# Layer two's last two query chunks of two tiles joined into one of four, with a second wide mixer buffer and new planning constants

## The chip, the cores and the metric

The kernel runs on one core of a Trainium2 chip. The metric is the time of one execution in device microseconds (us), less is better. A run is quoted as the median of its executions with their range. The span that a profile shows is of one of these executions (for the kernel before, of a further one), and about 1.8 us shorter than its timed value. The profiler also records the **granted clock** of TensorE, as a share of full speed: 1.00 or, for some microseconds at a time, 0.50.

## The reference, cut to what matters

```python
# x: 1 x 2048 x 448, bf16; 16 heads of 28; F = 1792
def _A_ref(x, wqkv, wo):                      # attention, all keys visible
    ...
    scores = einsum("bhqd,bhkd->bhqk", q, k) * Dh ** -0.5
    p = softmax(scores); o = einsum("bhqk,bhkd->bhqd", p, v)
    return o @ wo
def _B_ref(x, w1, w2, w3, w4):                # "mixer"
    h = gelu(layernorm(x) @ w1)
    # four quarters of h shifted by +1, -1, +2, -2 rows of the sequence
    x1 = x + concat(shifted quarters) @ w2
    return x1 + gelu(layernorm(x1) @ w3) @ w4
# twice: x = x + A(layernorm(x)); x = x + B(layernorm(x))
```

The sequence is 16 tiles of 128 rows. The row shifts are why a tile can be mixed only when its neighbour's attention is done: tiles 11-12 need tile 13.

## The kernel before

A list scheduler in Python plans every instruction before the kernel is built. Tasks (generators) offer operations with an assumed duration; the planner places each on its engine by priority and by the time at which it believes the inputs to be ready. **The order on each engine is fixed then.**

The softmax is a stream: TensorE writes score blocks into PSUM (the memory for its results, in eight banks), ScalarE takes two or three banks per exponential (1024 or 1536 columns), TensorE multiplies the result with the values. VectorE evaluates some 40 of the 2048 blocks itself with a polynomial. Projections and mixers are hidden beside this stream. What depends on the last query chunk comes after the last exponential; I call that the **tail**, and the end of the last exponential **T**.

```python
CHUNKS = {0: [...], 1: [(0, 4), (4, 4), (8, 4), (12, 2), (14, 2)]}    # (first tile, tiles) of query chunks, by layer
BGROUPS = {0: [...], 1: [[[0, 1, 2]], [[3, 4, 5, 6]], [[7, 8, 9, 10]], [[11, 12]], [[13, 14, 15]]]}  # mixers after each chunk
RANK = {...}      # order list of the hidden tasks
D_RATE = {...}    # how many blocks VectorE takes, by stage
Sched.TARGET = 0.64   # how dense TensorE is to be kept; the rest is filled with matmuls on the identity
Sched.DOUBT2 = {"dma": 1.5, "pool": 0.5, "dve": 0, "act": 0.7, "pe": 0.0}
# ... [cut]
    def ready_at(self, t, cand, reads, writes):
        for d in <producers of the inputs>:
            te = d.t_end + (0.2 if d.dma else ...)
            # ...
                elif eng in ("act", "dve"):
                    te += self.DOUBT2["dma" if d.dma else d.eng]      # a margin for what the planner doesn't know
```

The hidden layer of a mixer (14 pieces) has one full buffer, h2T; mixer 11-12 of layer two had a narrow one of its own; the mixers of the tail ("direct") use PT, which is free by then:

```python
            side = not direct and L == 1 and n == 2
            if direct:   hb = PT
            elif side:   hb = <256 columns per piece in vaug>
            else:
                yield ("acq", ["h2T"]); hb = h2T
            # w3 matmuls, copies to hb by VectorE, GELU by ScalarE, w4 matmuls
```

## Time and profile before

| | before |
|---|---|
| median (range) | 1076.44 us (1073.24 to 1077.02), 3 runs |
| profiled span, granted clock | 1074.8 us, 0.997 |
| ScalarE busy / idle between first exponential and T | 994.6 / 15.3 us |
| T, tail | 1027.3, 47.5 us |

A row of a timeline gives start, duration, engine, line, operation, output and inputs, shape and count; in brackets stands how long the engine was idle before it, and on what. A row of busy times by stretch gives the stretch, its length, then busy time and instruction count of each engine asked for, the granted clock, the share of DMA and its GB/s.

### The profile page before, as it was taken

Reading aid. Unit: us, or ns where it says so; the run is one execution under the profiler, and the core shown is the slowest. Engines: PE = TensorE matmul, PEld = TensorE weight load, DVE = VectorE, ACT = ScalarE, POOL = GpSimd, SP = SyncE. Lnnn points to the kernel's source line nnn. Section 1 sums busy time; section 2 is a strip of 40 time slices with the busy share of each in tenths; the row PEclk is TensorE's granted clock in tenths of the full one; section 3 lists DMA queues with packets and bytes.
Section 4 is the critical chain, followed back from the end, with each engine's and each line's share of the span. In section 5 each row is a group of like instructions: output and inputs, shape, how many; then the busy total and the mean of one; then the engine's idle time right before and its main releaser. Section 6 shows DMA issues by size and latency. Waiting matters only on the chain.

```text
span 1074.8 us, 35355 instructions
## 1 busy us (share of the span) xinstructions
PE 1010.3 (94%) x16037; PEld 422.5 (39%) x16037; DVE 619.8 (58%) x1236; ACT 1020.3 (95%) x920; POOL 312.9 (29%) x506
## 2 busy tenths in 40 slices
PE   7999999999999999999999998999999999999998
PEld 2333443443333433343433433353333433444455
DVE  7776569836468236765156553514797484444442
ACT  6898999999999999999999999999999999999952
POOL 2244125201254024452032201102743130432111
PEclk9999999999999999999999999999999999999999
DMA  4547221103111022120221123313411110220000
GB/s 115 138 110 208 83 57 32 24 17 91 32 32 32 13 78 56 44 42 22 63 58 40 41 85 95 133 50 110 89 27 21 43 39 16 59 49 16 12 11 32
DMA packets 95494, 62.26 MB, mean 58 GB/s; under 512 B 68528, under 2 KB 85248, under 8 KB 95344
## 3 DMA queue, kind: packets, MB, share of 16 engines
q1 hardware_dynamic: 91968, 51.92, 18.7%
q0 software_dynamic: 3376, 8.09, 2.7%
q8 instruction: 125, 2.05, 0.8%
q14 instruction: 25, 0.20, 0.1%
HBM read 27.12 MB, written 15.71 MB: 40 GB/s over the span
## 4 chain that ended last, share of the span: by engine, by line
ACT 72%; PE 18%; DVE 8%; issue 1%; DMA 0%; SPq 0%; DVEq 0%
ACT PT L1455 65%; PE ps L770 11%; ACT h2T L1852 4%; PE ps L1300 4%; PE ps L761 3%; ACT fb L1703 1%; ACT L1852 1%; DVE fb L1364 1%; DVE fb L1362 1%; ACT L1455 1%; DVE hT L1704 1%; DVE fb L1702 1%; DVE yd L1341 1%; DVE PD L1369 1%; DVE xn L962 0%
## 5 line engine op out<-in xcount | busy, mean ns | idle before, releaser
L1455 ACT ACTIVATE PT<-ps 128x1536 bf16<-128x1536 f32 (+1 forms) x805 | 920.8, 1339 | 14.2 <-PE ps L1300 13.2
L1300 PE MATMUL ps<-qT,kT 32*128 32x512 bf16 (+1 forms) x2560 | 315.0, 340 | 28.5 <-ACT PT L1455 19.8
L761 PE MATMUL ps<-PT,vaug 128*32 128x512 bf16 (+1 forms) x2523 | 250.3, 340 | 0.0
L1300 PEld LDWEIGHTS ps<-qT,kT 32*128 32x128 bf16 x2560 | 80.7, 91 | 300.6 <-ACT PT L1455 272.2
L1893 PE MATMUL ps<-ident 128*32 128x256 bf16 x3804 | 166.6, 274 | 3.4 <-POOL ident L850 1.5
L770 PE MATMUL ps<-xT,w 128*32 128x512 bf16 (+2 forms) x1600 | 126.5, 360 | 2.5 <-DVE h2T L1837 1.6
L1893 PEld LDWEIGHTS ps<-ident 128*32 128x32 bf16 x3804 | 107.8, 96 | 31.2 <-issue 12.3
L770 PE MATMUL ps<-w,h2T 128*32 128x448 bf16 x1512 | 106.3, 365 | 13.8 <-ACT h2T L1852 12.9
L1837 DVE CAST h2T<-ps 128x512 bf16<-128x512 f32 (+2 forms) x112 | 67.8, 606 | 79.5 <-PE ps L770 69.8
L761 PEld LDWEIGHTS ps<-PT,vaug 128*32 128x32 bf16 x2523 | 74.8, 95 | 93.4 <-issue 80.4
L1560 POOL TENSOR_TENSOR otn<-ub,fb 128x512 bf16<-128x512 f32 (+1 forms) x36 | 40.2, 1116 | 179.9 <-DMA fb<-rscr 179.7
L1096 POOL TENSOR_TENSOR sq<-kT 128x512 bf16<-128x512 bf16 (+2 forms) x32 | 29.9, 935 | 120.2 <-DVE kT L1110 120.0
L770 PEld LDWEIGHTS ps<-w,h2T 128*32 128x32 bf16 x1512 | 41.1, 98 | 51.7 <-issue 18.4
L1701 POOL TENSOR_TENSOR fb<-hT 112x512 f32<-112x512 bf16 (+1 forms) x36 | 37.5, 1044 | 79.2 <-DVE hT L1684 75.7
L770 PEld LDWEIGHTS ps<-xT,w 128*32 128x32 bf16 x1600 | 43.7, 95 | 42.6 <-issue 18.1
L1341 DVE TENSOR_SCALAR yd<-ps 128x512 int32<-128x512 f32 x37 | 25.1, 682 | 39.5 <-PE ps L1300 39.1
L1787 POOL TENSOR_TENSOR x_res<-x_res,x1b 128x448 f32<-128x448 f32 x32 | 38.9, 1222 | 20.9 <-DVE xn L967 20.8
L1534 DVE COPY ub<-ps 128x512 f32<-128x512 f32 (+1 forms) x40 | 23.3, 582 | 35.1 <-PE ps L761 34.8
L953 POOL TENSOR_SCALAR vpe<-mv 128x1 f32<-128x1 f32 (+2 forms) x21 | 5.5, 261 | 129.2 <-DVE mv L948 129.2
L1852 ACT ACTIVATE h2T<-h2T 128x7168 bf16<-128x7168 bf16 (+2 forms) x8 | 42.0, 5244 | 0.1
L1536 DVE SCALAR_TENSOR_TENSOR ub<-ub,fct,ps 128x512 f32<-128x512 f32 x24 | 17.9, 746 | 41.0 <-PE ps L761 40.7
L770 PE MATMUL ps<-kT,w 128*32 128x512 bf16 (+2 forms) x576 | 40.4, 360 | 1.1 <-DMA kT<-xn 1.0
(168 smaller groups left out, 1208.0 us busy)
## 6 DMA issues: line engine op xcount, KB each, us to landing
uscr<-ub SPq DMA_DIRECT2D x24, 256.0 KB
ub<-uscr SPq DMA_DIRECT2D x24, 256.0 KB
fb<-rscr SPq DMA_DIRECT2D x24, 256.0 KB
xnd<-xn SPq DMA_DIRECT2D x28, 128.0 KB, 2.2
x_res<-in_A_x_dram POOLq DMA_DIRECT2D x16, 224.0 KB, 4.0
xd<-x_res SPq DMA_DIRECT2D x16, 224.0 KB, 2.7
x_res<-xd SPq DMA_DIRECT2D x16, 224.0 KB, 3.0
out_dram<-obf SPq DMA_DIRECT2D x16, 112.0 KB
```

The source lines that it names most:

```text
L761: return lambda e: e.matmul(out=out, lhsT=lhsT, rhs=rhs, start=start, stop=stop, **kw)
L770: r.append(e.matmul(out=out[c:c + w, :], lhsT=lhsT[:, c:c + w], rhs=rhs, start=start, stop=stop, tile_position=(0, c)))
L1096: return op("pool", 0.15 + NW * 0.0018, lambda e: e.tensor_tensor(out=sq[:, si, 0:NW], in0=src, in1=src, op=ALU.mult), reads=rk, writes=[( ...
L1300: yield op("pe", max(0.055, 0.22 / nc_ * NW / 512.0), lambda e, i=i, kc=kc, j=j, g=g, a=a, NW=NW, bank=bank: e.matmul(out=ps[:, bank, i * ...
L1341: yield op("dve", c_ps(512), lambda e: e.tensor_scalar(out=y, in0=ps[:, bi(bank), :], scalar1=SCALE * L2E * FS, scalar2=-126.0 * FS, op0=A ...
L1455: yield op("act", 0.06 + n * w * 0.000833, lambda e, bk=bk, s0=s0, n=n, w=w: e.activation(out=PT[:, s0:s0 + n, 0:w], in_=ps[:, bk[0]:bk[0] ...
L1560: yield op("pool", 0.2 + NW * 0.0021, lambda e: e.tensor_tensor(out=otn[:, g, 0:NW], in0=u, in1=rb[:, 0:NW], op=ALU.mult), reads=[uk, fk], ...
L1701: yield op("pool", 0.2 + NW * 0.00165, lambda e: e.tensor_tensor(out=f, in0=z, in1=z, op=ALU.mult), reads=hk, writes=[fk])
L1787: yield op("pool", 1.2, lambda e: e.tensor_tensor(out=X, in0=X, in1=X1, op=ALU.add), reads=[xk, ("x1b", s)], writes=[xk], deps=[nop_])
L1837: ev = op("dve", c_ps(NW), lambda e, fch=fch, b=b: e.tensor_copy(out=hb[:, fch, 0:NW], in_=ps[:, bi(b), 0:NW]), reads=[("ps", bi(b))], wri ...
L1852: yield op("act", c_act(nl * NW), lambda e: e.activation(out=hb[:, 0:nl, 0:NW], in_=hb[:, 0:nl, 0:NW], func=ACT.Gelu_apprx_tanh), reads=al ...
L1893: return [e.matmul(out=ps[32 * c:32 * c + 32, bi(b), 0:256].rearrange("p (a n) -> p a n", n=128), lhsT=ident[:, 32 * c:32 * c + 32], rhs=i ...
```

## The change

The intent: fewer and larger steps at the end of layer two (512 columns instead of 256 for scores and value products of the last four tiles), and a second full-width mixer buffer so that hidden mixers don't wait for each other. With it ten rows of tuned constants were replaced.

```diff
-CHUNKS = {..., 1: [(0, 4), (4, 4), (8, 4), (12, 2), (14, 2)]}
+CHUNKS = {..., 1: [(0, 4), (4, 4), (8, 4), (12, 4)]}
-BGROUPS = {..., 1: [..., [[7, 8, 9, 10]], [[11, 12]], [[13, 14, 15]]]}
+BGROUPS = {..., 1: [..., [[7, 8, 9, 10]], [[11, 12], [13, 14, 15]]]}
-DPRIO = 5
+DPRIO = 1.5
-DSEG = 0
+DSEG = 1
-XSHUT = (10, 50)
+XSHUT = (20, 58)
-RANK = {... [('b', 0, 0), ('a', 0, 0), ('k', 0, 1), ('b', 0, 1), ... ]}
+RANK = {... [('b', 0, 1), ('b', 0, 0), ('a', 0, 0), ('k', 1, 0), ... ]}
-Q_LEAD = {(0, 1): 6, (0, 2): 9, (0, 3): 3, (1, 0): 7, (1, 1): 9, (1, 2): 4, (1, 3): 5}
+Q_LEAD = {(0, 1): 7, (0, 2): 7, (0, 3): 3, (1, 0): 7, (1, 1): 7, (1, 2): 4, (1, 3): 5}
-D_RATE = {(0, 0): 0.08, (0, 1): 0.05, (0, 2): 0.05, (0, 3): 0.06, (1, 0): 0.16, (1, 1): 0.1, (1, 2): 0.16}
+D_RATE = {(0, 0): 0.08, (0, 1): 0.045, (0, 2): 0.05, (0, 3): 0.045, (1, 0): 0.015, (1, 1): 0.1, (1, 2): 0.03}
-Sched.AGED = 0.1
-Sched.TARGET = 0.64
+Sched.AGED = 0
+Sched.TARGET = 0.6
-FTH = 0.03
+FTH = 0.15
-Sched.DOUBT2 = {"dma": 1.5, "pool": 0.5, "dve": 0, "act": 0.7, "pe": 0.0}
+Sched.DOUBT2 = {"dma": 1.5, "pool": 0.2, "dve": 0.5, "act": 0.5, "pe": 0.0}
 ... [cut: extra y/f/pd buffers for VectorE's blocks in free slots of vaug; a path for GpSimd blocks, with rate 0]
-                yield ("acq", [hname], [("xT", xt)])
-                hb, hkey = h2T, [[("h2T", f), ("xst",)] for f in range(14)]
+                hname = yield ("acq", ["h2T", "h2W"] if ("xdone", 1) in SC.events else ["h2T"], [("xT", xt)])
+                wide = hname == "h2W"        # 7 pieces in vaug, 7 in kT
 ... [cut]
```

## The prediction

> **What bounds the kernel now.** I read the busy shares and the chain first, then the costliest groups, then ScalarE's busy time in six stretches, then the timeline of the end.
>
> ```profile
> PE 1010.3 (94%) x16037; PEld 422.5 (39%) x16037; DVE 619.8 (58%) x1236; ACT 1020.3 (95%) x920; POOL 312.9 (29%) x506
> ACT 72%; PE 18%; DVE 8%; issue 1%; DMA 0%; SPq 0%; DVEq 0%
> ...
> L1455 ACT ACTIVATE PT<-ps 128x1536 bf16<-128x1536 f32 (+1 forms) x805 | 920.8, 1339 | 14.2 <-PE ps L1300 13.2
> ...
> L1893 PE MATMUL ps<-ident 128*32 128x256 bf16 x3804 | 166.6, 274 | 3.4 <-POOL ident L850 1.5
> ```
>
> ScalarE (ACT) holds 72% of the chain, with 805 softmax exponentials. TensorE is as busy on paper, but 166.6 us of it are matmuls on the identity that compute nothing and only keep it active. So the exponentials are the bound, as long as they run. ScalarE between the first exponential (17.34 us) and the end of the last (1027.27 us); columns are the stretch, its length, busy time:
>
> ```profile
> 17.34:100.00 82.66, 73.06 (x70) 1.00 0.48 123
> 100.00:300.00 200.00, 199.59 (x176) 1.00 0.22 57
> 300.00:500.00 200.00, 198.69 (x179) 0.99 0.16 39
> 500.00:700.00 200.00, 198.74 (x169) 0.99 0.24 71
> 700.00:900.00 200.00, 197.38 (x177) 1.00 0.22 52
> 900.00:1027.27 127.27, 127.15 (x109) 1.00 0.13 31
> sum 1009.93, ACT 994.62; mean ACT 165.77
> ```
>
> Idle is 1009.93 - 994.62 = 15.3 us: 9.6 in the first stretch, 2.6 between 700 and 900. Nothing else can be won in this stage but those 15.3 us and ScalarE's own work. After it comes a **tail** of another kind. First all engines (PE, PEld, DVE, ACT, POOL) from the last exponential to the end, then rows of its timeline (start, duration):
>
> ```profile
> 1027.30:1074.80 47.50, 44.59 (x848) 26.77 (x837) 17.46 (x36) 15.19 (x32) 9.72 (x21) 1.00 0.07 22
> ```
>
> ```profile
> 1031.38 1.70 PE L770 MATMUL ps<-wo_pad,otn 128*32 128x448 bf16 x32
> ...
> 1039.16 1.96 PE L761 MATMUL ps<-xT,w 128*112 128x256 bf16 x16
> ...
> 1047.68 2.06 PE L770 MATMUL ps<-w,h2T 128*32 128x448 bf16 x40
> ...
> 1052.77 9.28 PE L770 MATMUL ps<-kT,w 128*32 128x384 bf16 x224
> ...
> 1061.88 8.12 PE L770 MATMUL ps<-w,PT 128*32 128x448 bf16 x168
> ```
>
> Here TensorE is busy 44.59 of 47.5 us: output projection of two tiles (wo_pad), first mixer matmul (w, 256 columns), and the last three tiles' wide mixer (384 columns, then 168 of w4). In the gaps of this chain it works on what was left over: some 160 w4 matmuls of mixer 7-10 (the w,h2T row is one part; 160/4 x 0.193 us = 7.7 us) and most of mixer 11-12. That filling is what the change takes away.
>
> **What the Trainium skill says.** "ScalarE: Activation LUTs", section "What ACT_TABLE_LOAD costs": an activation with immediate scale takes 186 ns + 0.833 ns per column, a table load 1283 ns plus a drain of about 1380 ns. The trace has 6.18 us for 7168 columns (186 + 5971 = 6.16) and table loads of 1.28 us; the exponential before and the GELU after such a load stand directly beside it, so no separate drain of that size shows. "TensorE: Matmul & The Clock Gate", section "Wait — 56ns, not 53.3ns?": warm matmuls start N / 2.4 GHz + about 2.5 ns apart, and section "The mechanism" lets four column tiles run together. The trace agrees: 224 matmuls of 384 columns in 9.28 us are 166 ns per four (162.5 by the page). "Perfetto Trace Analysis", section "Identifying the Most-Contended Engine", says that TensorE's busy share is no good measure of how near it is to its limit; the 3804 idle matmuls here are a case of it.
>
> **Part 1: ScalarE's work.** By the instruction order of the changed kernel there are 401 exponentials of 1536 columns and 401 of 1024, against 402, 402 and one of 512. VectorE evaluates 43 score blocks, not 37 (2048 blocks in all). An unbroken pair takes 2.25 us in the chain of waits, so this saves 2.25 + 0.5 = 2.75 us. Four tanh of 256 columns leave the stream, since chunk four now ends in the tail: 0.31 us each as they stand between exponentials (an exponential starts 0.31 us after the tanh does), 1.25 us. Table loads and GELU columns stay: one GELU of 7168 becomes two of 3584, in the new buffer. Sum: **-4.0 us**, all on the path.
>
> **Part 2: idle time in the stream.** Retuned priorities can give back at most 15.3 us. In favour: the first wait of 4.0 us ends at 54.5 us behind two memsets on VectorE (0.24 and 0.81 us) and the queue at 45 to 54 us; the new order puts these behind the first bias update. From 772 to 814 us VectorE is the chain, with the twelve score blocks of layer two's third chunk among its work; that chunk's rate falls from 0.16 to 0.03, and the new order has five blocks there. On TensorE 512 score and 512 value matmuls of 256 columns become half as many of 512. Against: more blocks early, more conservative order. I take half, **-7.3 us**. The last exponential then ends at 1027.3 - 4.0 - 7.3 = 1016.0 us.
>
> **Part 3: the tail.** In the new order the GELU of mixer 7-10 stands 14 exponentials before the end, not 8, and all 224 w4 matmuls are placed ahead of the last value matmuls. Nothing is left over to fill gaps; identity matmuls stand there instead. And mixer 11-12 waits for chunk four. From the last exponential (T), with durations of the rows before:
> - value matmuls and copy of 512 columns: 0.5 + 0.69 = T+1.2. Normalisation: before, 2.77 us from copy to multiply; now four tiles, in two halves after each other (+0.5 for four more small matmuls, +1.4 for the second transpose, copy and spread) 4.7, then a multiply of 512 columns at 0.69: T+6.55. Before the projection began at T+4.1.
> - projection: 52 matmuls left, 2.75; last addition 0.7: T+10.0. Statistics of the first two tiles and the first aggregate: 1.25: T+11.3.
> - GpSimd makes the factors. Before, 8 small operations at 0.22 and 4 powers at 0.57 took 4.09 us (8 x 0.22 + 4 x 0.57 = 4.04). Up to the fourth tile's power there now stand 11 small ones and 6 powers: 5.84 us. Normalise, transpose, copy: 0.6 + 1.1. T+18.9 for the first mixer matmul, which was T+11.9 before.
> - that matmul: 64 of 512 columns, 16 x 0.22 = 3.5, last GELU 0.7: T+23.1.
> - second mixer matmul and second layer norm of tiles 11-12: VectorE 2 x 0.65 + 2 x 0.58 + 0.2, third tile 1.75, normalise 1.2, transposes and copies 1.5, waits 0.4: 7.5. T+30.6.
> - from here TensorE is full: w3 of 11-12, 56 plain matmuls at 0.116 (24 took 2.79) = 6.5; transposes 1.1; w4 112 / 4 x 0.193 = 5.4; w3 of 13-15 9.3; w4 8.1. Sum 30.4: T+61.0.
> - last subtraction and store: 2.9 as before (1071.9 to 1074.8). **T+63.9**, against T+47.5.
>
> Sum: 1016.0 + 63.9 = 1079.9 us of span; a timed run is 1.6 us longer (1076.44 against 1074.8): 1081.5. Since the waits in the tail are added in full and some will overlap, I put down **1078 us**.
>
> **The rivals.** First, the stream gains all its idle time: T = 1008, total 1072 to 1074. For it: the whole order was retuned. Against: the idle in the first 100 us comes from key projections and weights, which stay. Second, ScalarE waits more, since VectorE carries six more blocks at 3.43 us each (126.8 us over 37) and bank and buffer waits are new at the start; with 12 us of new idle instead of 7 less, 1097 us. For it: VectorE has 62.9 of 82.66 us busy early; against: it is at 65% or less in all later stretches. Third, the tail is bound by TensorE work and not by waits, as before; then it would be near 43 us of work plus 5, T+50, and the total 1066. Against: the listed order leaves only identity matmuls in the gaps at T+9 to T+19 and at T+24 to T+30. Fourth, the second wide buffer removes waits for h2T in layer two. TensorE's 12.9 us wait behind this GELU is largely beside a busy ScalarE, so it counts for nothing until the tail.
>
> **Range and chances.** Idle recovered from 0 to 15 us and a tail within 3 us give 1070 to 1091; the third rival pulls the low end down: **1066 to 1091 us**. Faster by over 2% needs less than 1054.9, below all of these: 0.03. Slower needs more than 1098, so 10 us of new idle: 0.05. Within 2%: 0.92.
>
> **What would show it.** Right: ScalarE's last exponential near 1016 us, 802 exponentials, a tail of 60 to 66 us, with identity matmuls between the output projection and the first mixer matmul, and a first mixer matmul of chunk four 7 us later after T than before. Wrong in part 2: idle in the stream still 15 us, or next to none. Wrong in part 3: the distance from the last exponential to the end below 57 us, or TensorE's identity matmuls absent there. Wrong altogether: exponentials that take another time each, or a chain in which ScalarE no longer holds some 70%.

## More of the kernel before

On the chip only semaphores decide when an instruction starts, never which one comes next.

The normalisation of a finished group of heads; `t` is the duration that the planner assumes for a transfer:

```python
                yield dma("sp", ... out=rT[0:16 * n, 0:32], in_=ub[28:128:32, ui, 0:NW] ..., t=1.9, iss=0.57)
                yield op("dve", 0.3, lambda e: e.reciprocal(out=rT[...], in_=rT[...]), reads=[("rT",)], writes=[("rT",)])
                # ... out to memory and back as a broadcast, then a multiply on GpSimd
```

## The result, and the profile after

| | before | after |
|---|---|---|
| median (range) of the first comparison | 1076.73 (1073.24 to 1079.48), 4 runs | **1116.50** (1109.81 to 1117.02), 4 runs |
| profiled span, granted clock | 1074.8, 0.997 | 1115.2, 0.977 |
| ScalarE busy / idle from first exponential to T | 994.6 / 15.3 | 994.0 / 33.9 |
| T, tail | 1027.3, 47.5 | 1045.1, 70.1 |

The changed kernel is **slower, ratio 1.0357** (95% interval 1.0307 to 1.0406). A ratio is the mean time of one kernel's runs over that of the other's in the same rounds, so it isn't quite the ratio of the medians. Of the 40.4 us between the two spans, 17.8 lie before T and 22.6 behind it; the profile is of the slowest of the four runs.

First the page of the changed kernel: busy shares, the shares of the chain that ended last, and the groups of the exponentials and of the identity matmuls (busy us, mean ns | idle before, what ended it).

```profile
PE 1026.4 (92%) x15450; PEld 416.9 (37%) x15453; DVE 631.1 (57%) x1250; ACT 1021.6 (92%) x917; POOL 306.5 (27%) x502
...
ACT 59%; PE 28%; DVE 7%; DMA 3%; POOL 2%; issue 1%; SPq 0%; DVEq 0%; POOLq 0%
...
L1534 ACT ACTIVATE PT<-ps 128x1536 bf16<-128x1536 f32 (+1 forms) x802 | 919.0, 1309 | 33.4 <-PE ps L1304 30.6
...
L1989 PE MATMUL ps<-ident 128*32 128x256 bf16 x3644 | 168.4, 279 | 8.3 <-DVE qT L1145 5.1
```

ScalarE's share of the chain fell from 72 to 59%, TensorE's rose from 18 to 28%. The exponentials themselves got 1.8 us cheaper (920.8 to 919.0). But ScalarE now waits 30.6 us for scores where it waited 13.2. One wait names another: TensorE's identity matmuls waited 5.1 us for VectorE's qT of line 1145. ScalarE's busy time in the same six stretches as before:

```profile
17.20:100.00 82.80, 73.99 (x71) 1.00 0.49 122
100.00:300.00 200.00, 191.65 (x168) 0.98 0.19 52
300.00:500.00 200.00, 195.96 (x176) 0.98 0.20 45
...
700.00:900.00 200.00, 193.93 (x174) 0.99 0.24 56
900.00:1045.10 145.10, 139.73 (x116) 0.94 0.09 23
sum 1027.90, ACT 993.98; mean ACT 165.66
```

Length less busy time: idle rose from 0.4 to 8.3 us between 100 and 300 us, from 1.3 to 4.0 in the next stretch, from 2.6 to 6.1 after 700 us and from 0.1 to 5.4 at the end, where the clock is 0.94. The largest single gap, on ScalarE (two more of 0.26 and 0.71 us follow it):

```profile
97.15 14.08 ACT L1534 ACTIVATE PT<-ps 128x1536 bf16<-128x1536 f32 x12
116.70 1.45 ACT L1534 ACTIVATE PT<-ps 128x1536 bf16<-128x1536 f32 x1 [5.47 <-PE ps L1304]
```

VectorE and TensorE at that time, each from its timeline:

```profile
107.36 0.69 DVE L1174 TENSOR_TENSOR qT<-qT,ps 128x512 bf16<-128x512 bf16 x1 [0.59 <-PE ps L771]
114.10 0.35 DVE L1628 RECIPROCAL rT<-rT 64x32 f32<-64x32 f32 x1 [6.05 <-DMA rT<-ub]
114.37 0.64 DVE L1145 TENSOR_SCALAR qT<-ps,bc 128x512 bf16<-128x512 f32 x1
```

```profile
115.07 1.04 PE L1989 MATMUL ps<-ident 128*32 128x256 bf16 x16 [5.11 <-DVE qT L1145]
```

VectorE stands 6.05 us in front of a reciprocal whose 8 KB transfer is late. Behind the reciprocal stands the evacuation of a q projection (L1145, its copy out of PSUM), whose data are ready. The next work on TensorE is 16 identity matmuls, which are to write a PSUM bank and wait for that evacuation, and the next scores stand behind them. So a wait on a small transfer goes through three engines into the softmax stream. Before, the two VectorE instructions stood the other way round:

```profile
107.54 0.75 DVE L1143 TENSOR_SCALAR qT<-ps,bc 128x512 bf16<-128x512 f32 x1 [1.74 <-PE ps L770]
111.72 0.34 DVE L1549 RECIPROCAL rT<-rT 64x32 f32<-64x32 f32 x1 [3.43 <-DMA rT<-ub]
```

There VectorE waited 3.43 us too, and nobody else did. In the changed kernel TensorE's pause also costs clock; its engines in stretches of 5 us (TensorE, its loads, VectorE, ScalarE, GpSimd, then the clock):

```profile
110.00:115.00 5.00, 0.00 (x0) 0.00 (x0) 0.90 (x2) 1.23 (x2) 0.00 (x0) 0.87 0.52 167
115.00:120.00 5.00, 4.93 (x53) 1.67 (x53) 0.70 (x2) 2.47 (x2) 1.04 (x1) 0.50 0.28 84
```

From 115 to 120 us TensorE is busy 4.93 of 5 us at half clock and feeds ScalarE for only 2.47. The Trainium skill, "TensorE: Matmul & The Clock Gate", section "What's actually happening", says that the clock falls to half after an idle window of about 3.4 us and returns after about as much sustained work. The trace agrees here: an idle stretch of some 5 us, then about 5 us at 0.50.

The tail, all engines in the same order:

```profile
1045.10:1115.20 70.10, 61.01 (x1128) 39.65 (x1120) 26.23 (x54) 17.11 (x36) 16.69 (x39) 0.90 0.04 12
```

It is 22.6 us longer than before, and its clock is 0.90.

### The profile page after: what moved, and what is told of

The parts are those of the page before. It is cut to its first block, busy times and chain, and to the rows that moved or that the text cites. A ratio compares the mean times of both kernels' runs of the same rounds, so it can differ in the third digit from the quotient of the medians.

```text
span 1115.2 us, 34183 instructions
## 1 busy us (share of the span) xinstructions
PE 1026.4 (92%) x15450; PEld 416.9 (37%) x15453; DVE 631.1 (57%) x1250; ACT 1021.6 (92%) x917; POOL 306.5 (27%) x502
## 3 DMA queue, kind: packets, MB, share of 16 engines
q1 hardware_dynamic: 88976, 50.84, 17.8%
## 4 chain that ended last, share of the span: by engine, by line
ACT 59%; PE 28%; DVE 7%; DMA 3%; POOL 2%; issue 1%; SPq 0%; DVEq 0%; POOLq 0%
ACT PT L1534 52%; PE ps L771 14%; PE ps L1304 7%; PE ps L762 6%; ACT h2T L1948 3%; DMA rT<-ub 1%; ACT fb L1782 1%; PE ps L1989 1%; ACT L1948 1%; ACT L1534 1%; DVE st L949 1%; DMA xT<-xnd 1%; DVE vaug L1386 0%; DVE PD L1431 0%; DVE xn L969 0%
## 5 line engine op out<-in xcount | busy, mean ns | idle before, releaser
L1534 ACT ACTIVATE PT<-ps 128x1536 bf16<-128x1536 f32 (+1 forms) x802 | 919.0, 1309 | 33.4 <-PE ps L1304 30.6
L771 PE MATMUL ps<-xT,w 128*32 128x512 bf16 (+2 forms) x1728 | 138.7, 376 | 2.7 <-issue 1.6
L1926 DVE CAST h2T<-ps 128x384 bf16<-128x384 f32 (+2 forms) x98 | 58.2, 594 | 76.2 <-PE ps L771 70.6
L771 PE MATMUL ps<-w,h2T 128*32 128x448 bf16 x1288 | 90.6, 355 | 10.0 <-ACT h2T L1948 9.9
L1780 POOL TENSOR_TENSOR fb<-hT 112x512 f32<-112x512 bf16 (+1 forms) x32 | 34.7, 1086 | 62.6 <-DVE hT L1763 56.9
L771 PEld LDWEIGHTS ps<-w,h2T 128*32 128x32 bf16 x1288 | 33.6, 96 | 41.4 <-issue 14.5
L771 PE MATMUL ps<-xT,wk_pad 128*32 128x512 bf16 (+2 forms) x576 | 44.9, 365 | 1.1 <-DVE kT L1112 0.6
L1714 POOL TENSOR_SCALAR mst<-mv 128x1 f32<-128x1 f32 x32 | 7.0, 220 | 135.8 <-DVE mv L950 133.9
L1098 POOL TENSOR_TENSOR sq<-qT 128x512 bf16<-128x512 bf16 x28 | 30.0, 1075 | 46.8 <-DVE qT L1145 40.2
L1974 DVE SCALAR_TENSOR_TENSOR obf<-x_res,shf,ps 128x448 bf16<-128x448 f32 x16 | 10.9, 680 | 55.6 <-PE ps L771 55.5
L771 PE MATMUL ps<-wo_pad,otn 128*32 128x448 bf16 x512 | 41.0, 369 | 1.1 <-DVE x_res L1693 0.9
L771 PE MATMUL ps<-xT,wq_pad 128*32 128x512 bf16 x448 | 38.9, 402 | 2.4 <-DMA xT<-xnd 1.6
```

The costliest lines, as they stand in the source:

```text
L771: r.append(e.matmul(out=out[c:c + w, :], lhsT=lhsT[:, c:c + w], rhs=rhs, start=start, stop=stop, tile_position=(0, c)))
L1098: return op("pool", 0.15 + NW * 0.0018, lambda e: e.tensor_tensor(out=sq[:, si, 0:NW], in0=src, in1=src, op=ALU.mult), reads=rk, writes=[( ...
L1534: yield op("act", 0.06 + n * w * 0.000833, lambda e, bk=bk, s0=s0, n=n, w=w: e.activation(out=PT[:, s0:s0 + n, 0:w], in_=ps[:, bk[0]:bk[0] ...
L1780: yield op("pool", 0.2 + NW * 0.00165, lambda e: e.tensor_tensor(out=f, in0=z, in1=z, op=ALU.mult), reads=hk, writes=[fk])
L1926: ev = op("dve", c_ps(NW), lambda e, hr=hr, vw=vw, b=b: e.tensor_copy(out=hr, in_=vw(ps[:, bi(b), 0:NW])), reads=[("ps", bi(b))], writes=h ...
```

## The experiments

First the sum of all kernels. Ratios are to the kernel before in the same rounds; T, tail and idle time (of ScalarE, first exponential to T) are from each one's single profile. All gave correct results.

| kernel | median (range) | ratio, 95% interval | T | tail | idle |
|---|---|---|---|---|---|
| old_tuning | 1096.28 (1093.49-1097.77) | 1.0188 (1.0168-1.0208) | 1027.2 | 64.5 | 15.8 |
| old_chunks | 1085.98 (1083.65-1086.67) | 1.0084 (1.0064-1.0103) | 1041.1 | 43.8 | 29.0 |
| tail_fill2 | 1114.41 (1108.81-1116.24) | 1.0343 (1.0310-1.0376) | 1039.2 | 67.9 | 28.5 |
| target75 | 1108.66 (1107.06-1109.06) | 1.0296 (1.0278-1.0313) | 1038.9 | 68.3 | 29.7 |
| recip_behind | 1105.98 (1101.68-1109.87) | 1.0274 (1.0249-1.0299) | 1037.2 | 67.0 | 25.9 |
| recip_ahead | 1080.90 (1078.53-1082.57) | 1.0040 (1.0022-1.0058) | 1033.3 | 47.5 | 20.0 |
| new_code_only | 1079.81 (1079.25-1081.73) | 1.0034 (1.0016-1.0052) | 1030.5 | 48.0 | 17.2 |
| doubt_old | 1119.75 (1114.82-1122.67) | 1.0398 (1.0368-1.0429) | 1049.6 | 65.5 | 38.7 |
| weights_later | 1109.62 (1104.65-1112.73) | 1.0304 (1.0278-1.0331) | 1041.3 | 67.0 | 29.8 |
| behind_fill | 1105.83 (1101.64-1109.14) | 1.0270 (1.0243-1.0297) | 1034.7 | 65.2 | 24.9 |
| one_buffer | 1102.36 (1096.92-1104.16) | 1.0231 (1.0199-1.0264) | 1034.2 | 65.0 | 20.9 |
| best_try | 1086.95 (1084.19-1090.97) | 1.0095 (1.0068-1.0123) | 1044.2 | 45.0 | 31.3 |
| groups_only | 1082.24 (1080.46-1083.11) | 1.0046 (1.0028-1.0063) | 1027.1 | 51.6 | 15.2 |
| rank_old | 1130.49 (1124.67-1133.97) | 1.0490 (1.0459-1.0522) | 1056.4 | 66.5 | 46.4 |
| before_fill | 1100.05 (1093.81-1104.08) | 1.0206 (1.0177-1.0236) | 1045.4 | 54.6 | 42.3 |

**1. Structure or constants: old_tuning and old_chunks.** My theory after the first reading was that two losses add: the structure lengthens the tail, and the retuned constants make the stream worse. The rival was that the structure itself disturbs the stream.

```diff
 # old_tuning: the changed kernel with the ten rows of constants of before
-DPRIO = 1.5 ... RANK, Q_LEAD, D_RATE, TARGET, FTH, DOUBT2 as changed
+DPRIO = 5 ...   RANK, Q_LEAD, D_RATE, TARGET, FTH, DOUBT2 as before
 # old_chunks: the changed kernel with CHUNKS, ORDER, BGROUPS (and the normalisation of the last chunk) of before
```

> The new chunks, mixer groups and buffers, with every tuning constant (priorities, leads, rates of VectorE's blocks, filler target, doubts) as before. If the structure costs the tail and the retuning costs the stream, the last exponential comes near 1028 us again (stream idle 15 to 20 us) and the tail stays at 64 to 70 us: 1093 to 1100 us. If the structure is all of the 40 us, about 1116 us; if the retuning is all, about 1077 us.

> The new tuning and new code, with layer two's chunks and mixer groups as before (two of two tiles). If the stream's extra 19 us of idle time belong to the retuning and the extra 23 us of tail to the structure, the tail is 46 to 50 us again and the last exponential stays late, near 1045 us: about 1095 us in all. If the structure is the cause of both, about 1077 us; if the retuning is, about 1115 us.

With the structure alone the stream of this profile is that of before: T is 1027.2 against 1027.3 and the idle time 15.8 against 15.3 us. The loss in it is the tail, 64.5 us instead of 47.5. By the ratio the loss is 20 us; the profile is of the fastest run, 2.8 us under the median. The engines in the tail, then the main groups of TensorE in it:

```profile
1027.20:1091.70 64.50, 55.51 (x1152) 35.92 (x1144) 26.53 (x55) 16.54 (x34) 17.26 (x39) 1.00 0.04 13
```

```profile
1033.79 2.64 PE L771 MATMUL ps<-wo_pad,otn 128*32 128x448 bf16 x52
...
1046.24 3.63 PE L771 MATMUL ps<-xT,w 128*32 128x512 bf16 x64 [0.19 <-DVE xT L995]
...
1071.58 9.27 PE L771 MATMUL ps<-xT,w 128*32 128x384 bf16 x224
1080.68 8.12 PE L771 MATMUL ps<-w,PT 128*32 128x448 bf16 x168
```

These are T+6.6, T+19.0, T+44.4 and T+53.5. With the constants alone the tail is 3.7 us shorter than before, but the stream idles 29.0 us, 13.7 more; at 1086 us it did better than the 1095 that I had expected. Both parts of the theory hold, but they don't add: by the ratios 1.88% and 0.84% make 2.72 of the measured 3.57%. The remaining 0.85%, some 9 us (3 to 15 by the three intervals), appears only when the new constants meet the new structure.

**2. The cold tail: tail_fill2.** In the changed kernel the tail is another 5.6 us longer than in old_tuning (70.1 against 64.5), at a clock of 0.90. Theory: TensorE is cold because there is too little to do around T.

```diff
+        for o in pe_ops[last_score:]:          # the plan is untouched
+            if <o is an identity matmul>:
+                o.fn = (lambda fn: lambda e: fn(e) + fn(e))(o.fn)     # issue it twice
```

> The changed kernel in the same order, with each identity matmul after the last score matmul issued twice (288 more). Clock theory: TensorE's clock, 0.90 in the tail, goes over 0.97 and the tail of 70.1 us shortens by 4 to 7 us, to 1110 us in all. Rival, that VectorE's and GpSimd's waits alone set the tail: it stays at 70 us or grows by up to 2 us.

The clock of the tail went to 1.00, and the tail shrank by only 2.2 us. The timed difference to the changed kernel isn't separated from zero (the intervals overlap). The 2.2 us aren't the worth of the clock, since the 288 added matmuls stand in front of useful work too. A better measure is recip_behind (experiment 4), whose tail has the very list of the changed kernel. The tails of tail_fill2 and of recip_behind:

```profile
1039.22:1107.10 67.88, 62.38 (x1416) 44.48 (x1408) 26.23 (x54) 17.13 (x36) 16.75 (x39) 1.00 0.04 13
1037.25:1104.20 66.95, 56.42 (x1128) 37.20 (x1120) 26.23 (x54) 17.12 (x35) 16.70 (x39) 0.97 0.04 12
```

The first mixer matmul starts at T+22.4 in the changed kernel (clock 0.90), at T+21.8 in tail_fill2 (1.00) and at T+19.5 in recip_behind (0.97). The same list takes 70.1 us at 0.90 and 67.0 at 0.97 (weights_later: also 67.0 at 0.97). A second pair with one list, target75 and behind_fill, has 68.3 at 0.95 and 65.2 at 1.00. So some 3 us go with 0.05 to 0.07 of clock; extended to 1.00, an estimate from these pairs, that is 4 to 6 us and may be all of the 5.6. The profile of tail_fill2 also shows how much one execution differs from the next: T is 5.9 us earlier than in the changed kernel, though nothing up to the last score differs. Single profiles are therefore good to some 6 us in T; the timed ratios decide.

**3. More identity matmuls throughout: target75.**

```diff
-Sched.TARGET = 0.6
+Sched.TARGET = 0.75
```

> The changed kernel with the scheduler's target for TensorE's activity at 0.75 for 0.6: 4764 identity matmuls for 3644. Clock theory: mean clock from 0.977 to 0.99 or more, stream idle from 34 to some 22 us, total 1095 to 1103 us. Rival, that the late transfers and not the clock make the idle time: the clock rises but the total stays within 4 us of 1116, or grows since identity matmuls stand in the way.

It gained: 1.0296 against 1.0357, though the intervals overlap by a little and the median of 1108.7 us lies between the two forecasts. Between 900 us and T the idle time fell from 5.4 to 0.2 us and the clock rose from 0.94 to 1.00. I took this for a clean test of the clock. It wasn't one: the planner counts identity matmuls in TensorE's time, so the order on the other engines moved too (by the traces VectorE's list of some 1240 instructions differs in about 300 places). It shows that such a plan exists, not that the clock alone made the difference.

**4. One pair of instructions: recip_behind and recip_ahead.** Theory: the gap at 110 to 120 us comes from the order of two VectorE instructions. The rival: the late transfer stops the stream anyway. Both edits exchange the pair after planning and touch nothing else; semaphores are recomputed from the new order.

```diff
 # recip_behind: the changed kernel
+        j = <first reciprocal of rT>; dve[j], dve[j + 1] = dve[j + 1], dve[j]   # q evacuation first
 # recip_ahead: the kernel before, the other way round
+        dve[j - 1], dve[j] = dve[j], dve[j - 1]                                 # reciprocal first
```

> The changed kernel with two neighbouring VectorE instructions exchanged and nothing else: the first reciprocal of rT, which waited 6.05 us for its transfer, now stands behind the q evacuation of line 1145 instead of ahead of it, as in the kernel before. Theory A (the longest gap of the softmax stream, 5.47 us of ScalarE at 116.7 us and 0.97 us in two more, comes from the order of these two instructions, and the half clock that follows is the consequence of TensorE's wait for the evacuation): the gap goes, the clock stays near 1 at 110 to 125 us, ScalarE's idle time between 100 and 300 us falls from 8.3 to about 1 to 2 us, and the last exp and the end come 6 to 7 us earlier, about 1109. Rival (the late transfer stops the stream anyway, through what waits for the reciprocal): the gap only moves by a few us and the time stays within 2 us of 1116.

> The control in the other direction: the kernel before with the same two instructions exchanged, its first reciprocal of rT (which waits 3.43 us for its transfer) put ahead of the q evacuation that came at 107.54 us. Theory A: the evacuation comes some 4 to 5 us later, TensorE waits for it, ScalarE's unbroken exps between 95 and 130 us get a gap of 3 to 6 us, and the time rises by 3 to 7 us, to about 1080 to 1084. Rival (the kernel before has slack there that the changed one lacks, the half clock is chance): less than 2 us.

In recip_behind VectorE still waits for the transfer, and ScalarE's exponentials run without a break (timelines of both):

```profile
107.91 0.75 DVE L1145 TENSOR_SCALAR qT<-ps,bc 128x512 bf16<-128x512 f32 x1 [0.18 <-PE ps L771]
113.22 0.34 DVE L1628 RECIPROCAL rT<-rT 64x32 f32<-64x32 f32 x1 [4.56 <-DMA rT<-ub]
```

```profile
96.83 33.50 ACT L1534 ACTIVATE PT<-ps 128x1536 bf16<-128x1536 f32 x29
```

In recip_ahead the gap appears in the kernel before, where there had been none; of the 6.0 us by which T is later, 4.2 are idle time between 100 and 300 us (timelines of VectorE and ScalarE):

```profile
111.54 0.34 DVE L1549 RECIPROCAL rT<-rT 64x32 f32<-64x32 f32 x1 [5.82 <-DMA rT<-ub]
111.81 0.64 DVE L1143 TENSOR_SCALAR qT<-ps,bc 128x512 bf16<-128x512 f32 x1
```

```profile
114.82 1.45 ACT L1455 ACTIVATE PT<-ps 128x1536 bf16<-128x1536 f32 x1 [3.12 <-PE ps L1300]
```

The exchange takes 10.5 us off the median of the changed kernel (8.9 by the ratios: 0.0083 of 1076) and, reversed, puts 4.3 us by the ratio on the kernel before. The theory holds in both directions, and the size in recip_behind is larger than the three gaps (6.4 us) by 2.5 us, which by the spread of T isn't more than chance could do.

**5. Why the transfer was late: weights_later.** The transfer of 8 KB was issued at 104.21 us beside the loads of w3 and w4 (3136 KB in three transfers, 313 GB/s between 105 and 110 us in the trace). Those aren't needed before some 200 us.

```diff
+        # after planning: the loads of w3 moved behind the fourth, of w4 behind the fifth multiply of line 1639 on GpSimd's list
```

> The changed kernel with the order of VectorE and TensorE untouched, but with the loads of w3 and w4 (1344 and 1568 KB, first needed at about 203 and 233 us), which were issued at 100.7 to 103.2 us, issued some 55 and 80 us later on the same queue. Theory: the 8 KB transfer into rT took 10 us because it ran beside these loads, where later ones of its kind take about 3.9 us from issue to the next step; so without them it lands at about 107 to 108, the reciprocal waits 1 to 2 us and not 6, the gap of 5.5 us in the softmax stream goes although the reciprocal still stands ahead of the q evacuation, and the time falls to 1104 to 1108, as with the two instructions exchanged. Rival (the transfer is late for another reason, or the loads stall a later step instead): the reciprocal still waits 4 us or more, or a new gap of some us opens between 155 and 240 us, and the time stays above 1112.

VectorE's timeline in weights_later, in the order of the changed kernel with the reciprocal still ahead of the evacuation, then ScalarE's:

```profile
108.06 0.34 DVE L1628 RECIPROCAL rT<-rT 64x32 f32<-64x32 f32 x1
108.33 0.75 DVE L1145 TENSOR_SCALAR qT<-ps,bc 128x512 bf16<-128x512 f32 x1
```

```profile
97.25 35.76 ACT L1534 ACTIVATE PT<-ps 128x1536 bf16<-128x1536 f32 x31
```

The reciprocal doesn't wait at all now: the transfer was issued at 104.31 us and takes at most 3.8 us, not 9.9. The gap goes. So the lateness was caused by the loads beside it. The planner had assumed 1.9 us, plus a margin of 1.5. The time fell by 6.9 us in the median, to a value between the two forecasts. The rival may have a small part: idle time between 100 and 300 us is 3.7 us where recip_behind has 2.9, and ScalarE waits 2.25 us at 198 us (clock 0.67 from 195 us, after the last load at its new place) where recip_behind waits 0.62. The interval of the ratio overlaps that of the changed kernel, so this timed gain is less sure than that of recip_behind.

**6. The new text alone: new_code_only.** Old chunks, old groups, old constants, new buffers.

```diff
 # old_tuning, and
-CHUNKS, ORDER, BGROUPS and the normalisation of the last chunk as changed
+CHUNKS, ORDER, BGROUPS and the normalisation of the last chunk as before
```

> The new program text (second wide buffer, extra buffers of VectorE's blocks) with the old chunks, the old mixer groups and the old constants. If chunking and constants together are the whole loss and the new buffers cost nothing: 1074 to 1080, T about 1027 and a tail of 44 to 47.5 us, so the same as before within 0.4%. If the extra buffers bring a gain by themselves (VectorE's blocks run earlier), up to 4 us faster. If they carry a part of the loss: above 1081.

It is 0.34% slower than before, in an interval that excludes zero. The extra buffers bring nothing by themselves; T is 3.2 us later, 1.9 of it idle time. So there is no gain here either.

**7. The margins alone: doubt_old.**

```diff
-Sched.DOUBT2 = {"dma": 1.5, "pool": 0.2, "dve": 0.5, "act": 0.5, "pe": 0.0}
+Sched.DOUBT2 = {"dma": 1.5, "pool": 0.5, "dve": 0, "act": 0.7, "pe": 0.0}
```

> The changed kernel with one row of constants as before: the margins that the planner adds to a producer's end before it places a waiting instruction (GpSimd 0.5, VectorE 0, ScalarE 0.7 us instead of 0.2, 0.5, 0.5). Its plan puts the first reciprocal behind the q evacuation again. If the stalls of the stream come from these margins: ScalarE's idle time in the stream falls from 33.9 to under 20 us and the time to about 1100. If the old margins only move the stalls to other places: idle time 25 to 35 us and 1108 to 1120. More than that would say that the rest of the constants was tuned around the new margins.

The gap at 115 us went as planned (idle time between 100 and 300 us is 0.7 us), and others opened: 8.5 us between 500 and 700 us and 12.2 between 700 and 900. The theory that this row carries the stalls falls. The time is no better than with the change.

**8. Both repairs: behind_fill.** The pair exchanged in target75's plan.

```diff
 # target75, and in its plan
+        dve[j], dve[j + 1] = dve[j + 1], dve[j]
```

> The changed kernel with both single repairs: the reciprocal behind the q evacuation, and the density of idle matmuls at 0.75 in place of 0.6 (the plan is otherwise the same). If the two causes are separate, they add: 1116.5 less 10.5 less 8 = 1098, with an idle time of the stream of about 20 us, and the clock between 900 us and the last exp at 1.0 instead of 0.93; that would be what the new chunks cost with the old constants (1096.3), and the interaction of structure and constants would be explained by the clock. If both work through the same clock and one repair leaves nothing to the other: 1104 to 1108.

The text says that the plan is otherwise the same as in the changed kernel; as told under target75, that is wrong. Measured against target75 the exchange gains 2.8 us by the ratios (0.0026 of 1077), which the overlapping intervals don't separate from zero; against recip_behind nothing is gained. So the repairs don't add, although the clock is 1.00 after 900 us and idle time there is 0.2 us: 5.3 us of idle time stand between 500 and 700 us and 5.3 after it, where recip_behind has 2.8 and 3.8.

**9. The second buffer: one_buffer.** On old_tuning, so that the constants play no part.

```diff
-                hname = yield ("acq", ["h2T", "h2W"] if ("xdone", 1) in SC.events else ["h2T"], [("xT", xt)])
+                hname = yield ("acq", ["h2T"], [("xT", xt)])
```

> The new chunks with the old constants, and the second wide mixer buffer never used, so that layer two's hidden mixers wait for the one buffer as before. If the second buffer is worth something with the new chunks: its w4 work of mixer 7-10 or the buffer wait pushes into the tail and the time is 3 to 8 us above that of the same kernel with two buffers (1096.3), so 1099 to 1104. If it is worth nothing, because only hidden work uses it: 1094 to 1098. If it costs: below 1094.

Without the second buffer T comes 7.0 us later and the tail is the same (65.0 against 64.5). Hence the buffer is worth about 5 us (0.0043 of 1077 = 4.6), inside the stream and not in the tail, as long as the chunks are the new ones. The intervals touch at their ends (1.0199 and 1.0208), so the size is rough.

**10. Group or chunk: groups_only.** The kernel before with mixer 11-12 moved to the end and nothing else.

```diff
-  1: [..., [[7, 8, 9, 10]], [[11, 12]], [[13, 14, 15]]]}
+  1: [..., [[7, 8, 9, 10]], [], [[11, 12], [13, 14, 15]]]}
```

> The kernel before, old chunks and old constants, with one part of the change alone: mixer 11-12 is taken out of the fourth chunk and runs with 13-15 at the end. By the steps of the prediction's third part the first mixer matmul of the last chunk stays at T+11.9, and from there everything is added: 2.7 for that matmul and its GELU, 7.5 to the second layer norm of 11-12, 30.4 of full TensorE, 2.9 for the store: T+55.4, so a span of 1082.7 and 1084.3 timed, if the grouping and the chunk of four share the 17 us of the tail as 8 to 9. If the grouping is nearly all of it: tail 60 to 65, 1088 to 1094. If the grouping costs nothing, because the old schedule did most of mixer 11-12 after the last exp anyway: tail under 51, 1076 to 1080.

```profile
1027.10:1078.70 51.60, 46.62 (x882) 30.11 (x875) 22.98 (x47) 15.07 (x33) 14.10 (x27) 1.00 0.06 20
```

The tail is 51.6 us: the moved group costs 4.1 us, and the chunk of four, with the new buffers, the other 12.9 (64.5 less 51.6; the new buffers alone leave the tail at 48.0 in new_code_only). T doesn't move with either (1027.1, 1027.2, before 1027.3), so no gain of the stream from the chunk of four shows in these profiles. The tail is shorter than the 55.4 us that I had worked out, since in the profile w4 matmuls of mixer 7-10 and w2 matmuls of 11-12 still find gaps to fill.

**11. The order list: rank_old.** All new constants except RANK and Q_LEAD.

```diff
 # the changed kernel
-RANK = {... [('b', 0, 1), ('b', 0, 0), ... ]}; Q_LEAD = {(0, 1): 7, (0, 2): 7, ... }
+RANK = {... [('b', 0, 0), ('a', 0, 0), ... ]}; Q_LEAD = {(0, 1): 6, (0, 2): 9, ... }
```

> The changed kernel with the order list of the hidden tasks and the lead of the q projections as before; all other constants stay new. The new constants cost 20 us on top of the new chunks. If the order list carries most of it: idle time in the stream under 22 us and 1095 to 1102. If the other constants (margins, rates and shutting points of VectorE's blocks, density of idle matmuls) carry it: idle time 28 us or more and 1110 to 1122. A value between says that both do.

It is the slowest kernel of all. Its idle time is 46.4 us, of which one gap is 17.8 us: ScalarE waits from 700 to 718 us for the first scores of layer two. So the new order list isn't what costs; together with the other new constants it is better than the old one. Rows of constants can't be judged one by one here.

**12. Attempts to beat both: best_try and before_fill.** best_try is old_chunks with the loads moved as in weights_later and TARGET at 0.75. before_fill is the kernel before with TARGET at 0.75.

```diff
 # best_try: old_chunks with the moved loads of weights_later, and
-Sched.TARGET = 0.6
+Sched.TARGET = 0.75
 # before_fill: the kernel before
-Sched.TARGET = 0.64
+Sched.TARGET = 0.75
```

> An attempt to beat both: the old chunks with the new constants (1086.0, whose tail was 3.7 us shorter than before), with the w3 and w4 loads issued later and the idle matmuls at 0.75. If the stall at 110 to 120 us (8.9 us of idle ScalarE there) and the half clock were all that cost it: 1086 less 8 less 2 = 1076, level with before within 3 us. If it keeps its other gaps (700 to 900 us, 6.7 us idle): 1078 to 1082. Under 1074 would beat both.

> A cheap attempt to beat both: the kernel before with the density of idle matmuls at 0.75 instead of 0.64. It has two cold spells, at 375 to 385 and 520 to 525 us, and its profile some 8 us at half clock. If these cost it time: 1073 to 1075. If they lie beside a ScalarE that is busy anyway, as its 1.3 us of idle time in each of those stretches says: 1075 to 1079, the same within the noise.

best_try is no faster than old_chunks: the gap at 110 to 120 us is gone, but 5.4 us opened between 500 and 700. before_fill is the larger surprise. One number that only asks for more identity matmuls made the tuned kernel 2% slower. ScalarE's timeline there:

```profile
684.21 15.02 ACT L1455 ACTIVATE PT<-ps 128x1536 bf16<-128x1536 f32 x13
713.55 10.06 ACT L1455 ACTIVATE PT<-ps 128x1024 bf16<-128x1024 f32 x9 [14.32 <-PE ps L1300]
```

A gap of 14.3 us stands where layer two begins. TensorE's first key projection there starts at 705.45 us after a wait that the profile names only as issue; the queue issued its last transpose of x at 699.8 us, where the plan before had issued its last one at 676.9. That the projection waited for this transpose is likely, and not shown. And between 100 and 300 us there are 6.9 us of idle time. No kernel that I tried beats the one before.

## Why the prediction was wrong

**The call.** It put 92% on a time within 2%, and the kernel is 3.6% slower.

**Part 1, ScalarE's work: small miss.** Count and shape of the exponentials were right. It put down -4.0 us; ScalarE's busy time up to T fell by 0.6 (994.6 to 994.0), and the exponentials' by 1.8. No gain of stream time shows: with the old constants T moved by 0.1 us.

**Part 2, idle time in the stream: this step failed.** It read the 15.3 us of idle time as a store from which "retuned priorities can give back" something, between none and all, and took half. What the runs showed in its place is +18.6 us. The wait that it named at 54.5 us did go (ScalarE's gap near it is 0.72 us now), yet the first stretch still idles 8.8 of its 9.6 us, and others came, of which the largest is the 5.5 us behind the reciprocal. With the two short gaps after it that is 6.4 us; the rest of the new idle time, between 300 and 500 us and after 700, has no cause shown. Shown by exchange in both kernels: one pair of neighbours decides over a gap of 3 to 6 us. Shown by weights_later: the cause of the wait is a transfer of 8 KB that took 9.9 us beside bulk loads where the planner reckons with 1.9 us and a margin. The order list was inspected for counts; whether something short stood behind something that waits for a transfer was not.

The error of thought is in the range. 15.3 us wasn't an average from which one goes up or down alike; it was the outcome of tuned constants. The experiments give the spread: edits that kept the old constants have 15.2 to 20.9 us of idle time (old_tuning, groups_only, new_code_only, one_buffer, recip_ahead), while those with new or changed constants have 24.9 to 46.4. The second rival had the right sign and direction, "12 us of new idle", but its first cause (VectorE's additional blocks) isn't what the largest gap shows; its second (waits for banks and buffers at the start) is nearer, since that gap is a wait for a PSUM bank.

**Part 3, the tail: right in mechanism and, with the old constants, in size.** It put the projection at T+6.55, the first mixer matmul at T+18.9, and from its sums the last w3 at T+43.6 and the end at T+63.9. Measured in old_tuning: T+6.6, T+19.0, T+44.4, T+64.5. In the changed kernel itself the end is T+70.1. Most of the 5.6 us above go with the clock of 0.90 (experiment 2): recip_behind, with the very same list of instructions in its tail, has 67.0 at 0.97. The prediction reckoned with warm durations throughout; what made the tail cold isn't settled. The division was wrong by its own steps: they gave the moved group 8 us (55.4), where groups_only measured 4.1.

**The sum.** In the profiles: predicted T 1016.0 and tail 63.9; measured 1045.1 and 70.1. So 29.1 us of the miss are part 1 and 2, 6.2 the tail, and the rounding down from 1081.5 to 1078 adds 3.5. Without the gain of part 2 its steps give 1088.8 us; the structure alone (old_tuning) measured 1096.3, and the 4.0 us of part 1 are most of that difference. The prediction's own sign of being "wrong altogether", a chain in which ScalarE no longer holds some 70%, came true: 59%.

**What stays open.** The 5.4 us of idle time between 900 us and T go with a low clock, and target75 and behind_fill have neither; as their plans differ, the cause is argued, not shown. Why structure and new constants together lose some 9 us more than each alone is explained in part: the pair costs 8.9 us in the changed kernel, but the same gap stands in old_chunks (5.19 us at 118.7), so it isn't of the interaction only. Which of the numeric constants matters most wasn't separated; rank_old and doubt_old say that single rows can't be judged alone.

## What to carry to other kernels

With a planner that fixes the order at build time, a change of constants is a new kernel: measure the structure with the old constants first, and treat the little idle time that tuning has left as probably near its low end, not as something that a retune gives back. When reading a plan, look on each in-order engine for an instruction that waits for a transfer, and ask what stands behind it and whom that holds up; put short work whose inputs are ready ahead of it, and keep bulk loads that aren't needed soon away from small transfers that are. An edit that is made after planning (exchange a pair, move a load, issue something twice) tests one cause; an edit of a planner's constant tests a whole new plan.

## What the Trainium skill lacked or had wrong

- "DMA: Bandwidth & Descriptors", section "Queues, rings and completion order", says that each DMA engine takes turns between the queues it has work for, one packet at a time. That gives no warning of what was seen: an 8 KB transfer issued at 104.21 us beside loads of 3136 KB from another queue was followed by its reader at 114.10, and at 108.06 at the latest without those loads. A figure for the delay of a small transfer beside a bulk load is lacking.
- "TensorE: Matmul & The Clock Gate", section "What's actually happening", ties half clock to an idle window of about 3.4 us. It fits at 110 to 120 us of the changed kernel. That section doesn't explain the following stretches of recip_behind, from its engines in steps of 5 us: the clock is 0.50 from 970 us on, while between 960 and 970.8 us no gap of TensorE above 0.21 us shows in its timeline; small fp32 matmuls stand at its start. The page's section "A second HAM failure mode: psum-queue depth-cycling" tells of frequent short idles as another way to a changing clock; TensorE was busy 4.74 and 4.79 us in the two stretches of 5 us before. No run here isolates the cause.

```profile
970.00:975.00 5.00, 5.00 (x35) 1.97 (x27) 0.56 (x2) 3.58 (x4) 0.00 (x0) 0.50 0.00 0
975.00:980.00 5.00, 5.00 (x35) 1.49 (x32) 1.38 (x2) 3.78 (x3) 0.00 (x0) 0.50 0.00 0
```

- No page gives a measured cost of half clock for a kernel that another engine bounds: in these two stretches ScalarE was busy 3.58 and 3.78 of 5 us, so some 2.6 us were lost in 10 us at half clock; in the tail, the same list of instructions took 70.1 us at a clock of 0.90 and 67.0 at 0.97.
